# Partial results added by adding transfers instead of on VectorE, and a later start of two lines of dense work, in an FNet and Mish-dense mix

## The chip, the cores and the metric

The kernel runs on one core of a Trainium2 chip. That core has TensorE (PE) for matrix products, VectorE (DVE) for elementwise work, ScalarE (ACT) for copies and activations, GpSimd (POOL) and SyncE (SP), which here only issue transfers between the chip's DRAM and its SBUF, and 16 DMA engines that carry those transfers out. PE writes its sums into PSUM, which has eight banks of 128x512 floats. The metric is the device time of one execution in microseconds (us); less is better.

## The reference

The input is x of 2048 rows (the sequence) by 640 columns. Two branches of it are mixed, row by row, by a gate:

```python
g = _sigmoid((x * gate_w).sum(-1, keepdims=True))
# branch A: real part of a Fourier transform over both axes
a = jnp.einsum("bsd,ed->bse", x, dft_hid_re)
b = jnp.einsum("bsd,ed->bse", x, dft_hid_im)
y = jnp.einsum("ts,bse->bte", dft_seq_re, a) - jnp.einsum("ts,bse->bte", dft_seq_im, b)
# branch B: dense, Mish, dense (640 -> 1728 -> 640)
h = jnp.einsum("bsd,df->bsf", x, w1) + b1
sp = jnp.log1p(jnp.exp(-jnp.abs(h))) + jnp.where(h > 0, h, jnp.zeros_like(h))
act = h * jnp.tanh(sp)
return g * y + (1 - g) * jnp.einsum("bsf,fd->bsd", act, w2)
```

All of it is in float32.

## The kernel before

**Products.** Every matrix product is cut into tiles of 128x128 by 128x512. To keep float32 accuracy each operand is split into a high and a low part: ACT copies the tile into a rounded type (the groups that the profile calls `cut<-flat` on ACT, lines 521 and 529), and DVE subtracts that from the tile to get the rest (`cut<-flat,cut` on DVE, all of whose elementwise work is recorded by line 483). A product is then three matmuls, high by high, high by low and low by high (`mm3`, which calls `mm`; every matmul of the kernel has line 535). Operands that are sums or differences of tiles are built first, on DVE (`flat<-flat`), since the large products are taken in a scheme with fewer products and more additions, of Strassen's kind, at two levels.

**Stages.** The sequence transform is made first, on x itself, as four problems `sq[0]` to `sq[3]`: the even ones (0 and 2) with the real matrix (`in_c_re_dram`) and the odd ones (1 and 3) with the imaginary one (`in_c_im_dram`), and of each pair the first for one half of the result and the second for the other. A problem has a `first`, a `second` and a `third` part. The first parts of all four come ahead. While they run, work of the first dense layer is laid between their steps: two lists of units (`lines`), each unit a few matmuls with `in_w1h_dram` and `in_xt_dram`, an activation and a store. In a loop over the 23 steps of the first parts of problems 2, 3 and 0, the first list gives one piece per step from the first step on, the second from the second step on; what is left of the lists is given behind the loop. Then, for q = 0 to 3, come the second and third part of `sq[q]` and a **second-level unit** (class `Halves`). The units of q = 0 and 1 (`UNITS`) make a sum of their own and hand three tiles of 128x512 on to the problem `sq[q + 2]`, whose own three tiles wait in DRAM (`ps`, its `aside`). The units of q = 2 and 3 (`LOWER`) hand three tiles to `sq[q - 2]`, whose three wait in DRAM too (`pl`, its `lower`). After the four come the gate, the hidden transform (`hd`), the second dense layer (`fin`, `ou`) and the output.

**How a second-level unit adds before the change.** In `Halves.steps`, `self.y(0, t2)` loads a partial tile from DRAM into an SBUF tile (SP issues it), DVE adds the unit's PSUM bank to it (`tt(r21, p4, r21, OP.add)`), the second half of the unit runs, a second PSUM bank is added, and the result is stored by POOL as a tile of `u`, the sequence transform's result in DRAM. Three tiles go this way in each unit (lines 957 to 959 and 992 to 994), so each unit has three loads, three DVE additions that are there for the loaded tile alone, and three stores.

**Adding transfers.** POOL can issue a transfer that adds what it carries to what lies at its destination. The kernel uses it already: `add_in` (line 495) adds a second tile of the Fourier matrix from DRAM to one in SBUF; in the trace these are `flat<-in_c_im_dram` and `flat<-in_c_re_dram` on POOL.

**What sets the order.** Everything is first recorded in a graph and then ordered by a planner (`run`, `order`). PE's order is the order of the code. The orders of DVE, ACT, SP and POOL and the choice of buffers come from the planner, which simulates the engines with its own durations and gives each piece a due time (`want`). Before the change it makes 12 tries from random seeds (`TURNS`), each from the best one so far, and keeps the one in which PE loses least by the plan. Stores and adding transfers all stand in POOL's one queue, and loads in SP's.

```python
def add_in(v, src):
    dma("POOL", lambda: nc.gpsimd.dma_start(v.t, src, accum_op=OP.add), whole(v), whole(v), ADDED * P * N * 4)
```

Of the kernel before, what the change touches and what calls it, by code (L numbers as in the profile page):

```python
# [17 lines left out]
P = 128  # L18
# [25 lines left out]
ADDED = 2.0  # L44
BEHIND = 9
# [29 lines left out]
class Graph:  # L75
# [73 lines left out]
    def run(self, pools):  # L149

        self.wants()
        full = [list(p.free) for p in pools]
        vals = {id(v): v for op in self.ops for v in op.vals}.values()
        left = [v.left for v in vals]
        best = None
        for turn in (None, *TURNS, "last"):
            if best:
                for op, want in zip(self.ops, best[1]):
                    op.want = want
            if best and turn != "last":  # L160
                rng = Random(turn)
                if rng.random() < 0.5:
                    self.adapt(best[2], rng.choice((2.0, 4.0, 8.0)), rng.choice((0.3, 0.6, 1.0)))
                self.hurry(best[2], rng)
            wants = [op.want for op in self.ops]
# [8 lines left out]
            began = self.order(pools, turn == "last")  # L174
            if not began or turn == "last":
                continue
            lost = max(began[op.n] - op.at for op in self.ops if op.engine == "PE")
            if not best or lost < best[0]:
                best = lost, wants, began

    def hurry(self, began, rng):

        def sooner(op, want):
            todo = [(op, want)]
            while todo:
                op, want = todo.pop()
                want = max(want, op.since)
                if op.engine == "PE" or want >= op.want:
                    continue
                op.want = want  # L190
                todo += [(d, want - d.took) for d in op.deps]
        last = None
        for op in self.ops:
            if op.engine != "PE":
                continue
            if last and began[op.n] - began[last.n] > MM + TOLD and rng.random() < 0.7:
# [31 lines left out]
    def order(self, pools, final):  # L228
# [69 lines left out]
        while left:  # L298
            went = False
            for e, line in ready.items():  # L300
# [92 lines left out]
def fnet_mish_gate(ctx: ExitStack, tc: tile.TileContext, xn, xt, c_re, c_im, wd_re, wd_im,  # L393
# [99 lines left out]
    def add_in(v, src):  # L493

        dma("POOL", lambda: nc.gpsimd.dma_start(v.t, src, accum_op=OP.add), whole(v), whole(v), ADDED * P * N * 4)  # L495

# [147 lines left out]
    class Problem:  # L644
# [3 lines left out]
        def __init__(self, st, tp, moving, finish, y=None, q=None, rest=None, aside=None, last=False, apart=None, bare=False, lower=None):  # L648
            self.st, self.moving, self.finish, self.y, self.q = st, moving, finish, y, q
            self.t1, self.t2, self.rest, self.aside, self.last = 2 * tp, 2 * tp + 1, rest, aside, last  # L650
            self.apart, self.bare, self.lower = apart, bare, lower
            self.held, self.kept = {}, [Val(t=dr.tile([P, N], F32, name=f"s2_{next(serial)}")) for k in range(st.kh)]
# [27 lines left out]
        def second(self, low):  # L680
# [10 lines left out]
            for p, k in in_turn(kh, *[("s3", "s2", "s1")] * 2, ends):  # L691
                if ("s3", k) not in own and p == ("s3" if k < kh - 2 else ends[0]):
                    low(k)
                    a22 = self.moving(t2, k + kh)
                    summed = st is seq and k in SUMMED
# [182 lines left out]
    class Halves:  # L878
# [35 lines left out]
        def steps(self):  # L914
# [72 lines left out]
            if not self.into:  # L987
# [4 lines left out]
                f = self.y(4, t2)  # L992
                tt(f, d2, f, OP.add)
# [427 lines left out]
    def put_out(d, t, f, queue=None):  # L1421
# [5 lines left out]
                  lower=aside(f"pl{q}") if q + 2 in LOWER else q in LOWER) for q in range(4)]  # L1427
    hd = [Problem(hid, tp, lambda t, k: load_of(FS, usc[k][t]), put_y, aside=None,
# [33 lines left out]
    for q in range(4):  # L1462
        sq[q].second(seq.low)
        sq[q].third()
        if q in UNITS:
            later = sq[q + 2]
            unit = Halves(seq, 0, 2, lambda t, k: c_tile(q)(t, k + KH), None, sq[q],
                          lambda d, t: load_of(FS, later.aside[min(d, 2)]), later.finish)
# [3 lines left out]
        if q in LOWER:  # L1472
# [3 lines left out]
                          lambda d, t: load_of(FS, there.lower[min(d, 2)]), there.finish, True)  # L1476
# [85 lines left out]
```

## Time and profile before

| | before |
|---|---|
| time, median of 3 runs | 845.81 us (845.71 to 846.83) |
| time of the profiled execution | 847.53 us |
| span of its trace, first to last instruction | 845.8 us |
| granted TensorE clock, mean | 0.999 |

The profiled execution is 1.7 us longer than the median, which is its own variation and what lies around the span; a sum made in its trace is set against 847.53, and its difference carried to 845.81. Engines are named as above; `PEld` is PE's loading of weights, which runs beside its matmuls, `SPq` and `POOLq` are the two queues that issue transfers. A timeline row has the start, the length, the engine, line, operation, output and inputs of a stretch of like instructions, how many (x), and in square brackets how long the engine was idle ahead of it and what ended that. The rows are shown where the prediction uses them.

### The profile page before, as it was taken

To read this page: it belongs to the slowest core of one execution; us is meant where nothing else is said; L and a number is where in the kernel's file an instruction comes from. 1 tells how busy PE (TensorE), PEld (TensorE's weight loads), DVE (VectorE), ACT (ScalarE), POOL (GpSimd) and SP (SyncE) were. 2 spreads that over 40 slices of the span, in tenths; PEclk is the share of its full clock that TensorE was granted. 3 is DMA by queue.
4 is the path that set the end of the run, shared out by engine and by line. 5 is a ranking of instruction groups with operands and counts; after the bars stand their busy time and mean duration, and the time that the engine had idled before them with its cause. 6 is when DMAs were issued, how large, how long until landed. Compare 5 with 4: busy or idle time off the path is not lost.

```text
span 845.8 us, 12270 instructions
## 1 busy us (share of the span) xinstructions
PE 838.9 (99%) x3679; PEld 689.3 (82%) x3679; DVE 759.8 (90%) x1204; ACT 544.3 (64%) x1016; POOL 142.4 (17%) x239
## 2 busy tenths in 40 slices
PE   9999999999999999999999999999999999999998
PEld 6788888878888888888888878888888888888886
DVE  6966989999899999999999999998585899999984
ACT  6966775875475566657658767656576886645442
POOL 0133230112111301220010022012233111011200
PEclk9999999999999999999999999999999999999999
DMA  9979998899789986998667959778799798969963
GB/s 307 354 260 355 324 303 265 273 299 334 231 295 280 349 270 202 301 340 291 181 218 243 328 201 390 228 255 272 251 306 409 268 311 280 341 193 315 301 224 144
DMA packets 120228, 238.77 MB, mean 282 GB/s; under 512 B 15264, under 2 KB 23328, under 8 KB 120160
## 3 DMA queue, kind: packets, MB, share of 16 engines
q1 hardware_dynamic: 98912, 177.80, 62.3%
q0 software_dynamic: 21104, 60.05, 22.9%
q8 instruction: 29, 0.48, 0.2%
q14 instruction: 39, 0.32, 0.1%
q10 hardware_dynamic: 144, 0.13, 0.0%
HBM read 183.64 MB, written 54.28 MB: 281 GB/s over the span
## 4 chain that ended last, share of the span: by engine, by line
PE 71%; DVE 13%; issue 7%; DMA 5%; POOL 2%; SPq 1%; ACT 0%; POOLq 0%; DVEq 0%; ACTq 0%
PE ps L535 71%; DVE cut L483 7%; DVE flat L483 5%; DMA flat<-in_c_re_dram 2%; SPq L456 1%; DMA flat<-in_c_im_dram 1%; DMA flat<-early 1%; POOL act L466 1%; DMA act<-flat 1%; DMA u<-flat 1%; DVE ps L483 1%; DMA flat<-in_xt_dram 1%; POOL flat L495 0%; POOL early L466 0%; POOL t L623 0%
## 5 line engine op out<-in xcount | busy, mean ns | idle before, releaser
L535 PE MATMUL ps<-cut 128*128 128x512 f32 x3671 | 835.4, 389 | 2.0 <-DVE cut L483 0.9
L535 PEld LDWEIGHTS ps<-cut 128*128 128x128 f32 x3671 | 688.3, 188 | 149.5 <-DVE cut L483 2.7
L529 ACT ACTIVATE cut<-flat 128x512 fp32r<-128x512 f32 x499 | 298.8, 627 | 198.1 <-DVE flat L483 122.1
L483 DVE TENSOR_TENSOR cut<-flat,cut 128x512 fp32r<-128x512 f32 (+5 forms) x551 | 400.0, 757 | 28.0 <-ACT cut L529 24.8
L483 DVE TENSOR_TENSOR flat<-flat 128x512 f32<-128x512 f32 (+4 forms) x439 | 281.5, 665 | 9.0 <-DMA flat<-in_c_im_dram 3.4
L509 ACT ACTIVATE flat<-ps 128x512 f32<-128x512 f32 x171 | 99.3, 595 | 49.9 <-PE ps L535 42.4
L483 DVE TENSOR_TENSOR flat<-ps,flat 128x512 f32<-128x512 f32 x123 | 81.3, 685 | 26.6 <-PE ps L535 23.2
L521 ACT ACTIVATE cut<-flat 128x256 fp32r<-128x256 f32 (+4 forms) x190 | 85.0, 478 | 12.8 <-DVE flat L483 8.3
L509 ACT ACTIVATE ps<-flat 128x512 f32<-128x512 f32 x74 | 43.4, 594 | 6.4 <-DVE flat L483 5.1
L466 POOL DMA_DIRECT2D act<-flat x52 | 28.2, 542 | 96.0 <-ACT flat L1018 74.6
L466 POOL DMA_DIRECT2D u<-flat x40 | 22.1, 556 | 108.7 <-ACT flat L509 53.9
L1018 ACT ACTIVATE flat<-flat,b1s 128x512 f32<-128x512 f32 x33 | 23.8, 721 | 12.5 <-DVE flat L483 12.1
L483 DVE TENSOR_TENSOR ps<-ps,flat 128x512 f32<-128x512 f32 x35 | 23.4, 694 | 3.2 <-ACT flat L509 2.1
L495 POOL DMA_DIRECT2D flat<-in_c_im_dram x16 | 14.0, 877 | 68.3 <-DVE cut L483 22.3
L495 POOL DMA_DIRECT2D flat<-in_c_re_dram x16 | 14.4, 922 | 41.7 <-DMA flat<-in_c_re_dram 25.3
L1018 ACT ACTIVATE flat<-ps,b1s 128x512 f32<-128x512 f32 x19 | 13.0, 687 | 8.1 <-PE ps L535 7.0
L471 POOL DMA_DIRECT2D out_dram<-flat x10 | 8.8, 970 | 51.4 <-DMA flat<-act 26.9
L466 POOL DMA_DIRECT2D out_dram<-flat x10 | 5.4, 539 | 51.8 <-DVE flat L483 51.4
L1392 DVE SCALAR_TENSOR_TENSOR flat<-flat 128x640 f32<-128x640 f32 x16 | 13.1, 818 | 0.7 <-DMA flat<-in_xn_dram 0.7
L466 POOL DMA_DIRECT2D s<-flat x12 | 6.5, 546 | 41.4 <-DVE flat L483 21.1
L466 POOL DMA_DIRECT2D y<-flat x10 | 5.4, 540 | 45.4 <-DVE flat L483 44.7
L466 POOL DMA_DIRECT2D early<-flat x12 | 6.7, 562 | 26.0 <-ACT flat L509 11.1
(36 smaller groups left out, 73.3 us busy)
## 6 DMA issues: line engine op xcount, KB each, us to landing
flat<-in_c_im_dram SPq DMA_DIRECT2D x112, 256.0 KB, 5.0
flat<-in_c_re_dram SPq DMA_DIRECT2D x112, 256.0 KB, 4.8
flat<-act SPq DMA_DIRECT2D x88, 256.0 KB, 5.4
flat<-u SPq DMA_DIRECT2D x60, 256.0 KB, 4.9
act<-flat POOLq DMA_DIRECT2D x52, 256.0 KB, 4.7
flat<-in_xt_dram SPq DMA_DIRECT2D x42, 256.0 KB, 4.7
u<-flat POOLq DMA_DIRECT2D x40, 256.0 KB, 5.6
flat<-in_xn_dram SPq DMA_DIRECT2D x24, 320.0 KB, 4.6
```

What stands on the lines that cost most here:

```text
L456: op = dma(queue, lambda: ISSUE[queue].dma_start(v.t[:rows, :cols], src() if callable(src) else src), whole(of) if of else [], whole(v), r ...
L466: dma(queue, lambda: ISSUE[queue].dma_start(d.t, v.t[:rows]), whole(v), whole(d), rows * N * 4)
L471: dma("POOL", lambda: nc.gpsimd.dma_start(o.t, v.t, accum_op=OP.add), whole(v, o), whole(o), 2.8 * P * N * 4)
L483: nc.vector.tensor_tensor(o, a, b, op=alu)
L495: dma("POOL", lambda: nc.gpsimd.dma_start(v.t, src, accum_op=OP.add), whole(v), whole(v), ADDED * P * N * 4)
L509: act(lambda: nc.scalar.activation(o.t, a.t, AF.Copy, scale=scale), whole(a), whole(o))
L521: act(lambda: nc.scalar.activation(w.t[0][:, c], src.t[:, s], AF.Copy), whole(src), hs, n)
L529: act(lambda: nc.scalar.activation(r.t[0][:, :N], src.t[:, :N], AF.Copy), whole(src), [(r, 0)])
L535: G.add("PE", lambda: nc.tensor.matmul(bank.t, w.t[wn][:, k * P:k * P + P], x.t[xn_][:, :N], start, stop, skip_group_check=True), [(w, (k, ...
L1018: act(lambda: nc.scalar.activation(o.t[rows], src.t[rows], AF.Mish, **more), whole(src, table) + whole(b1s) * bias, whole(o), more=0.1)
L1392: dve(lambda k=k, x=x: nc.vector.scalar_tensor_tensor(x.t, x.t, 1.0, wide.t, op0=OP.mult, op1=OP.mult, accum_out=gcol.t[:, k:k + 1]), whol ...
```

## The change

The change has four parts. First, the units of q = 0 and 1 no longer load the partial tile: `self.y` is `None`, ACT copies the PSUM bank to SBUF (`to_sbuf`), and at the end `onto` issues an adding transfer (`add_in` with the DRAM tile as its source) into that SBUF tile, ahead of the store. Second, the unit of q = 2 does not load either: the three tiles of `sq[0]` are stored in their places in `u` from the start, and the unit's results are added to them there by POOL (`add_to_dram`). The unit of q = 3 (`PLAIN`) is as it was. Third, the two lists of first dense units begin at steps 1 and 2 instead of 0 and 1 (`BEGIN`). Fourth, the planner takes the eight new seeds one upon another and uses the last, and counts transfers of the plan's first 60 us as 1.08 times as long (`SLOW`).

```diff
+SLOW = 60.0, 1.08
+BEGIN = 1, 2
-TURNS = (120000, 120002, 120003, 120005, 120008, 120012, 120021, 120029, 120045, 120049, 120056, 120057,)
+TURNS = (700003, 700004, 700006, 700007, 700011, 700013, 700017, 700065)
+PLAIN = (3,)
...
-        for turn in (None, *TURNS, "last"):
...
+        began = again(not TURNS)
+        for turn in TURNS:
+            self.haste(began, turn)
+            began = again(turn == TURNS[-1])
...
-                    dma = max(now + DELAY, dma) + op.moves
+                    dma = max(now + DELAY, dma) + op.moves * (SLOW[1] if now < SLOW[0] else 1)
...
-        o = place(d, t)
+        add_to_dram(place(d, t), v)
+
+    def add_to_dram(o, v):
+
         dma("POOL", lambda: nc.gpsimd.dma_start(o.t, v.t, accum_op=OP.add), whole(v, o), whole(o), 2.8 * P * N * 4)
...
-    def add_in(v, src):
-
-        dma("POOL", lambda: nc.gpsimd.dma_start(v.t, src, accum_op=OP.add), whole(v), whole(v), ADDED * P * N * 4)
+    def add_in(v, src, of=None):
+
+        dma("POOL", lambda: nc.gpsimd.dma_start(v.t, of.t if of else src, accum_op=OP.add),
+            whole(v, of) if of else whole(v), whole(v), ADDED * P * N * 4)
...
-                r21, r22 = self.y(0, t2), self.y(1, t2)
-                tt(r21, p4, r21, OP.add)
-                tt(r22, b, r22, OP.add)
+                if self.y:
+                    r21, r22 = self.y(0, t2), self.y(1, t2)
+                    tt(r21, p4, r21, OP.add)
+                    tt(r22, b, r22, OP.add)
+                else:
+                    r21, r22 = to_sbuf(p4), to_sbuf(b)
...
-                f = self.y(4, t2)
-                tt(f, d2, f, OP.add)
+                if self.y:
+                    f = self.y(4, t2)
+                    tt(f, d2, f, OP.add)
+                else:
+                    f = to_sbuf(d2)
...
-                  lower=aside(f"pl{q}") if q + 2 in LOWER else q in LOWER) for q in range(4)]
+                  lower=(aside(f"pl{q}") if q + 2 in PLAIN else [usc[q % 2 * KD + j][1] for j in (0, 1, 4)]) if q + 2 in LOWER else q in LOWER) for q in range(4)]
...
-        for line in lines if n else lines[:1]:
-            next(line, None)
+        for line, start in zip(lines, BEGIN):
+            if n >= start:
+                next(line, None)
...
-            unit = Halves(seq, 0, 2, lambda t, k: c_tile(q)(t, k + KH), None, sq[q],
-                          lambda d, t: load_of(FS, later.aside[min(d, 2)]), later.finish)
+
+            def onto(d, t, v):
+                add_in(v, None, later.aside[min(d, 2)])
+                later.finish(d, t, v)
+            unit = Halves(seq, 0, 2, lambda t, k: c_tile(q)(t, k + KH), None, sq[q], None, onto)
...
-                          lambda d, t: load_of(FS, there.lower[min(d, 2)]), there.finish, True)
+                          (lambda d, t: load_of(FS, there.lower[min(d, 2)])) if q in PLAIN else None,
+                          there.finish if q in PLAIN else lambda d, t, v: add_to_dram(there.lower[min(d, 2)], v), True)
```

What the planner makes of this is seen in the engines' orders, of which three places follow. Each row is a line of the source, an operation, its output and input, its shape, and how many of it follow one another.

The first place is SP's queue from its 14th transfer (13th after the change) to its 28th, issued before in the first 18 us: loads of Fourier matrix tiles (`in_c_im`, `in_c_re`), of x (`in_xn`) and of the first dense layer's operands (`in_xt`, `in_w1h`). Before:

```order
L456 DMA flat<-in_xn_dram 128x384
L456 DMA flat<-in_xt_dram 128x512 x3
L456 DMA flat<-in_w1h_dram 128x384 x2
L456 DMA flat<-in_c_im_dram 128x512
L456 DMA flat<-in_xt_dram 128x512
L456 DMA flat<-in_w1h_dram 128x384 x2
L456 DMA flat<-in_c_im_dram 128x512
L456 DMA flat<-in_xn_dram 128x384
L456 DMA flat<-in_c_re_dram 128x512 x3
```

And after the change:

```order
L457 DMA flat<-in_c_im_dram 128x512 x2
L457 DMA flat<-in_xt_dram 128x512 x2
L457 DMA flat<-in_w1h_dram 128x384
L457 DMA flat<-in_xt_dram 128x512
L457 DMA flat<-in_xn_dram 128x384
L457 DMA flat<-in_xt_dram 128x512
L457 DMA flat<-in_c_im_dram 128x512
L457 DMA flat<-in_w1h_dram 128x384 x2
L457 DMA flat<-in_xn_dram 128x384
L457 DMA flat<-in_w1h_dram 128x384
L457 DMA flat<-in_c_re_dram 128x512 x3
```

The last `in_c_im` ahead of the three `in_c_re` had four `in_w1h` ahead of it and has one now; the last `in_xn` had four and has three. The `in_xn` before that one, which was the 14th transfer, is the 19th.

The second place is PE at the end of the loop over the first parts, some 100 us into the program, where the rest of the two lists is given out. `ps` and a number is a PSUM bank; a bank's rows are the matmuls that add into it. Before:

```order
L535 MATMUL ps_69<-cut 128x512 x6
L535 MATMUL ps_74<-cut 128x512 x3
L535 MATMUL ps_72<-cut 128x512 x3
L535 MATMUL ps_68<-cut 128x512 x3
L535 MATMUL ps_73<-cut 128x512 x6
L535 MATMUL ps_69<-cut 128x512 x3
L535 MATMUL ps_71<-cut 128x512 x15
```

And after:

```order
L540 MATMUL ps_74<-cut 128x512 x3
L540 MATMUL ps_68<-cut 128x512 x3
L540 MATMUL ps_67<-cut 128x512 x3
L540 MATMUL ps_73<-cut 128x512 x6
L540 MATMUL ps_70<-cut 128x512 x6
L540 MATMUL ps_73<-cut 128x512 x3
L540 MATMUL ps_72<-cut 128x512 x15
```

Before, the bank that six matmuls fill (`ps_69`) is taken up again for three after fifteen others; after the change (`ps_73`) after six others.

The third place is POOL's queue around the end of the unit of q = 0, some 200 us into the program. `u_` and numbers are tiles of the result in DRAM, `ps_` and a number partial tiles in DRAM. Before:

```order
L495 DMA flat<-in_c_im_dram 128x512 x4
L466 DMA u_0_78<-flat 128x512
L466 DMA u_0_94<-flat 128x512
L466 DMA u_2_80<-flat 128x512
L466 DMA u_2_84<-flat 128x512
L466 DMA u_2_96<-flat 128x512
L466 DMA u_0_82<-flat 128x512
L495 DMA flat<-in_c_im_dram 128x512 x4
```

And after:

```order
L499 DMA flat<-in_c_im_dram 128x512 x4
L467 DMA u_0_78<-flat 128x512
L467 DMA u_0_94<-flat 128x512
L499 DMA flat<-in_c_im_dram 128x512
L499 DMA flat<-ps_251 128x512
L499 DMA flat<-ps_252 128x512
L499 DMA flat<-ps_253 128x512
L467 DMA u_0_82<-flat 128x512
L499 DMA flat<-in_c_im_dram 128x512
L467 DMA u_2_80<-flat 128x512
L467 DMA u_2_84<-flat 128x512
L499 DMA flat<-in_c_im_dram 128x512
```

The second group of four additions to the Fourier tiles is taken apart: its first two have changed places, and the one that PE needs first, the first of the four before, now stands behind one other such addition, the three new adding transfers and one store, with the three stores that they feed behind it.

More of the change, by code (lines that the diff above doesn't have):

```diff
@@ L44 @@
 ADDED = 2.0
+SUMMED_HID = 0
+PLAIN = (3,)
 BEHIND = 9
@@ L154, in run, with again @@
         left = [v.left for v in vals]
-        best = None
-        for turn in (None, *TURNS, "last"):
[L157 to L165, printed above, removed]
+        def again(final):
             for p, free in zip(pools, full):
@@ L173, in run, with haste, hurry @@
                 op.mate = None
[L174 to L181, printed above, removed]
+            return self.order(pools, final)
+        began = again(not TURNS)
+        for turn in TURNS:
+            self.haste(began, turn)
+            began = again(turn == TURNS[-1])
+    def haste(self, began, turn):
+        rng = Random(turn)
+        if rng.random() < 0.5:
+            self.adapt(began, rng.choice((2.0, 4.0, 8.0)), rng.choice((0.3, 0.6, 1.0)))
+        self.hurry(began, rng, 0.7)
+    def hurry(self, began, rng, share):
         def sooner(op, want):
@@ L195, in hurry @@
                 continue
-            if last and began[op.n] - began[last.n] > MM + TOLD and rng.random() < 0.7:
+            if last and began[op.n] - began[last.n] > MM + TOLD and rng.random() < share:
                 o, by = op, rng.choice((0.5, 1.0, 2.0, 4.0, 8.0))
@@ L651, in __init__ @@
             self.apart, self.bare, self.lower = apart, bare, lower
+            self.summed = SUMMED if st is seq else range(SUMMED_HID) if st is hid and not tp else ()
             self.held, self.kept = {}, [Val(t=dr.tile([P, N], F32, name=f"s2_{next(serial)}")) for k in range(st.kh)]
@@ L694, in second @@
                     a22 = self.moving(t2, k + kh)
-                    summed = st is seq and k in SUMMED
+                    summed = k in self.summed
                     if summed:
@@ L1426, in fnet_mish_gate @@
                   apart=UNITS and q % 2 in UNITS, bare=q - 2 in UNITS,
[L1427 to L1428 removed]
+                  lower=(aside(f"pl{q}") if q + 2 in PLAIN else [usc[q % 2 * KD + j][1] for j in (0, 1, 4)]) if q + 2 in LOWER else q in LOWER) for q in range(4)]
+    hd = [Problem(hid, tp, lambda t, k, v=None: add_in(v, None, usc[k][t]) if v else load_of(FS, usc[k][t]), put_y, aside=None,
                   q=lambda t: keep(("g", t), lambda: broadcast(grow, t))) for tp in range(2)]
```

## The prediction

> **What bounds the kernel now.** I begin with the page's first lines, for the share of each engine.
>
> ```profile
> span 845.8 us, 12270 instructions
> PE 838.9 (99%) x3679; PEld 689.3 (82%) x3679; DVE 759.8 (90%) x1204; ACT 544.3 (64%) x1016; POOL 142.4 (17%) x239
> ```
>
> PE is busy 99% of the span, so the question is how much PE loses and where. The timeline of PE lists its unbroken stretches; a stretch of the chain of waits from 275 us on gives its pace when nothing is late.
>
> ```profile
> 0.78 3.57 PE L1370 MATMUL ps<-const-bfloat16-1.0 128*128 128x512 bf16 x8 [0.78 <-PEq L1550]
> 4.39 6.76 PE L535 MATMUL ps<-cut 128*128 128x512 f32 x28
> 11.38 10.27 PE L535 MATMUL ps<-cut 128*128 128x512 f32 x44 [0.23 <-DVE cut L483]
> 21.98 1.12 PE L535 MATMUL ps<-cut 128*128 128x512 f32 x2 [0.33 <-ACT cut L521]
> 23.82 151.93 PE L535 MATMUL ps<-cut 128*128 128x512 f32 x669 [0.71 <-DVE cut L483]
> 176.03 323.80 PE L535 MATMUL ps<-cut 128*128 128x512 f32 x1425 [0.28 <-ACT flat L509]
> 500.08 341.61 PE L535 MATMUL ps<-cut 128*128 128x512 f32 x1503 [0.26 <-ACT flat L509]
> 274.98 25.16 PE ps L535 x111
> ```
>
> 111 matmuls in 25.16 us is 0.2267 us each. The stretches hold 3671 matmuls, 832.2 us at that pace; begun at 4.39 they would end at about 836.8 (the last one's own pipeline adds 0.16), and they end at 500.08 + 341.61 = 841.69. So PE loses **4.9 us in all**, 0.58% of the time: no change that leaves PE its matmuls can win more, and this one leaves all 3671. From start to start the loss is, stretch by stretch: 0.64 up to 11.38 (6.99 us for 28); 0.63 up to 21.98 (10.60 for 44) and 1.39 up to 23.82 (1.84 for 2), together 2.02 at **the start**; 0.55 up to 176.03; 1.00 up to 500.08; 0.72 from there on. Shorter waits within the long stretches show in the loading of weights, which stands idle far beyond its usual gap:
>
> ```profile
> 183.65 1.47 PEld L535 LDWEIGHTS ps<-cut 128*128 128x128 f32 x7 [0.44 <-DVE cut L483]
> 193.08 0.99 PEld L535 LDWEIGHTS ps<-cut 128*128 128x128 f32 x5 [0.24 <-DVE cut L483]
> 501.74 1.23 PEld L535 LDWEIGHTS ps<-cut 128*128 128x128 f32 x6 [0.43 <-ACT flat L509]
> 621.27 0.76 PEld L535 LDWEIGHTS ps<-cut 128*128 128x128 f32 x4 [0.41 <-DVE flat L483]
> ```
>
> Thus of the 1.00 up to 500.08 some 0.45 lies at 183.65 and 193.08 and 0.55 at 500.08 itself; the 0.72 lies at 501.74 and 621.27. DVE, busy 90%, is what ends most of these waits, but they are short: it is a second bound, not the first.
>
> **The change, part by part.**
>
> *The nine additions.* The groups by line give the prices:
>
> ```profile
> L535 PE MATMUL ps<-cut 128*128 128x512 f32 x3671 | 835.4, 389 | 2.0 <-DVE cut L483 0.9
> ...
> L529 ACT ACTIVATE cut<-flat 128x512 fp32r<-128x512 f32 x499 | 298.8, 627 | 198.1 <-DVE flat L483 122.1
> ...
> L483 DVE TENSOR_TENSOR flat<-ps,flat 128x512 f32<-128x512 f32 x123 | 81.3, 685 | 26.6 <-PE ps L535 23.2
> ...
> L509 ACT ACTIVATE flat<-ps 128x512 f32<-128x512 f32 x171 | 99.3, 595 | 49.9 <-PE ps L535 42.4
> ...
> L509 ACT ACTIVATE ps<-flat 128x512 f32<-128x512 f32 x74 | 43.4, 594 | 6.4 <-DVE flat L483 5.1
> ```
>
> Three units lose three DVE additions each, 9 x 0.685 = 6.2 us of DVE, and ACT gains nine copies, 9 x 0.595 = 5.4 us at 64% load. Nothing of this lies on PE's path by itself, since PE is unbroken beside nearly all of it. It is worth something only at waits on DVE that come later: 0.72 at 501.74 and 621.27 (the first names ACT, whose copies there wait in turn on DVE's sums; I count it in). The waits at 176.03, 183.65 and 193.08 (0.55 + 0.45) lie ahead of the first removed addition and can only move by the new plan. The 0.55 at 500.08 is a copy from a bank that PE has just filled, in code that the change leaves: it stays. I take 0.7 for the later waits, half of the 1.0 for the earlier, and give back 0.2 for waits that a new plan makes elsewhere: **-1.0**, between -1.7 (all gone) and +0.3 (none gone, some new).
>
> *The start.* The loss of 2.02 is the last pair of a Fourier tile and an x tile of the first part, which come late:
>
> ```profile
> 11.69 0.97 SPq L456 DMA_DIRECT2D flat<-in_w1h_dram  x2
> ...
> 13.92 0.97 SPq L456 DMA_DIRECT2D flat<-in_w1h_dram  x2
> 15.26 0.33 SPq L456 DMA_DIRECT2D flat<-in_c_im_dram  x1
> 15.90 0.33 SPq L456 DMA_DIRECT2D flat<-in_xn_dram  x1
> ...
> DMA packets 2684, 4.21 MB, mean 351 GB/s; under 512 B 422, under 2 KB 1267, under 8 KB 2684
> ...
> flat<-in_c_im_dram SPq DMA_DIRECT2D x3, 256.0 KB, 4.7
> ...
> 21.87 1.89 DVE L483 TENSOR_TENSOR cut<-flat,cut 128x512 fp32r<-128x512 f32 x5
> ```
>
> The tile issued at 15.26 lands 4.7 us later, at about 20.0, the x tile at about 20.5; ACT's cuts follow, and DVE's for the x tile is the last of the five in the row at 21.87, done at 23.76, when PE goes on. In the new order the Fourier tile has one `in_w1h` load ahead of it instead of four, the x tile three instead of four. At 351 GB/s, 192 KB take 0.56 us, so the first comes 1.7 us sooner, the second 0.56; fewer small dense cuts stand ahead of the x tile's on DVE, since dense work begins a step later. The x tile still lands at about 19.9, and its ACT cut, DVE cut and what stands between reach PE about 1.0 us sooner than now: I take **-1.0**, between -0.4 (only the sooner x tile) and -2.0 (all of it). Against it stands the x tile of the step before, now the 19th load: the load in that place is the second in the row at 11.69, issued by 12.7 and landed near 17, while PE is held up only by the last pair, at 21.3, so I cost it at nothing; if that cover is gone, the gain at the start shrinks with it. The 0.64 at 11.38 stays, since the first twelve loads are the same.
>
> *The later start of the two lists* leaves more for the end of the loop, near 106 us. There a bank is summed on DVE, set again by ACT and filled on by PE. The chain is a matmul from issue to end, 0.389 by its group, the DVE sum, 0.685, and the ACT copy, 0.594: 1.67 us. PE had fifteen other matmuls meanwhile, 3.4 us; it has six, 1.36, and with the last one's own slot 1.59. Bare, that is 0.1 short; with three hand-overs I take **+0.35**, from +0.1 to +0.9 if DVE has just begun another 0.685 us instruction.
>
> *The adding transfers.* The first row below is the share of the DMA engines in use, in tenths, from 198 to 222 us; then come the two queues in 212.6 to 223.2, where just three adding transfers ran beside loads, the time from issue to landing of such transfers from 180 to 230, and rows of POOL and DVE.
>
> ```profile
> DMA  9999999999999999999899999999999999999999
> ...
> q1 hardware_dynamic: 1348, 2.45, 63.7%
> q0 software_dynamic: 432, 0.79, 40.3%
> ...
> DMA to landing us min/median/max: 5.5/6.9/7.5
> ...
> 205.68 0.91 POOL L495 DMA_DIRECT2D flat<-in_c_im_dram  x1 [1.56 <-DMA flat<-in_c_im_dram]
> ...
> 204.84 0.81 DVE L1392 SCALAR_TENSOR_TENSOR flat<-flat 128x640 f32<-128x640 f32 x1
> ...
> 215.61 1.89 DVE L483 TENSOR_TENSOR cut<-flat,cut 128x512 fp32r<-128x512 f32 x3
> ```
>
> An adding transfer takes 40.3% of 10.6 us by three, 1.42 us of all 16 DMA engines; a load (2.45 MB is 9.35 tiles) 0.72. In each of units 0 and 1 three loads (-2.2) give way to three adds (+4.3); in unit 2 three loads and three stores give way to three adds, which is nothing. So the chip's DMA has 4.2 us more to do, most of it where it is already full, around 200 to 220. The place that counts is the Fourier addition issued at 205.68, landed by the median at 212.6. It now stands behind four adds that stood behind it or were not there (+5.7) and ahead of three stores (-2.2); the three loads are gone (-2.2); and POOL may reach it up to 1.7 sooner. That puts it at 212.2 to 213.9, and I take 213.2. Behind it come ACT's cut, 0.63, and in DVE's queue some six instructions that follow each other at 0.60 (the row at 215.61) and two of the gate at 0.74: 5.7 us, so PE's matmul can go at 218.9. It is the 190th behind the one at 176.03 and due at 219.5 (190 x 0.2267 and 0.4 for the waits at 183.65 and 193.08), or some 0.6 sooner after the gains ahead: 218.9. It is a tie, and I take **+0.5** from 0 to +2.3, and **+0.1** for units 1 and 2, where PE ran unbroken beside the additions (the row at 274.98), with up to +0.5.
>
> The Trainium skill, "DMA: Bandwidth & Descriptors", section "Issuing engines are not separate DMA queues", speaks against this part: transfers started by any engine run on the same 16 DMA engines and interleave, so a second queue saves only the time of issuing. The trace agrees: 63.7% and 40.3% share one whole. By that page the adds could only delay the loads, which would be the slower rival below.
>
> **The sum** is -1.0 - 1.0 + 0.35 + 0.5 + 0.1 = -1.05 us. Made in the profiled execution, 847.53 with a span of 845.8, it would give 846.5; the median of the runs shown is 1.7 lower, which I take as that execution's own variation around the same steps. Carried to the median, 845.81 - 1.05 is **844.8**.
>
> **The rivals.**
>
> *Covers hold and the gaps close.* The start gains 1.7, the drain costs 0.2, the adds nothing, the other waits give 1.4: -2.9, **842.9**. For it: DVE has 6.2 us less to do from 200 us on and fewer dense cuts at the start; PE waits on DVE in five of the nine waits shown. Against it: the x tile comes only 0.56 sooner.
>
> *It does not matter.* PE is at 99% and the removed work lay beside it; the plan trades one small wait for another. Start -0.5, drain +0.4, adds +0.3, rest -0.2: **845.8**. For it speaks that each of the losses is below 2.1 us and of its own cause.
>
> *Slower: the Fourier addition behind the adds.* If it lands past 213.2 on POOL's queue, each further us is PE's. With no earlier issue and half the relief from the three loads it lands at 215.0 (212.6 + 5.7 - 2.2 - 1.1), so +1.8; the same arrangement in unit 1, where PE had more lead, adds 0.7; the drain at 0.9 and a start that gains 0.9 cancel, and the rest gives nothing: +2.5, **848.3**. Against it: three of the loads that crowd this place are gone.
>
> **How the numbers follow.** I give the forecast 0.38 (844.0 to 845.7), the closed gaps 0.30, no matter 0.20, the late addition 0.12. A measurement of this kernel can tell about 0.2%, 1.69 us: below 844.12 is faster, above 847.50 slower. The closed gaps lie below the first bound and a sliver of the forecast's (0.04) does: **faster 0.34**; the rest of it and the third case: **same 0.54**; **slower 0.12**. The ends of all terms add up to -3.6 and +3.6; with about a tenth left out on each side the range is **842.8 to 847.3**.
>
> **What would show it.** PE's timeline of the changed kernel should have one loss near 22 us, of about 1 us instead of 2.02, a small new one near 105 us with ACT's copy to a bank as its end, no waits near 621, and the one near 500 as before. Near 219 it has a wait of 0 to 1 us that DVE's cut ends; 2 us there is the slower rival. The DVE group `flat<-ps,flat` should count nine fewer and ACT's `flat<-ps` nine more. I am wrong if a loss of over 1 us stands at a place not named here, or if the last x tile of the start comes no sooner.

## The result and the profile after

The changed kernel takes **854.06 us** (median of 4 runs, 853.03 to 855.58) against 846.32 for the kernel before in the same session (845.71 to 847.52): a ratio of 1.0091 with a 95% interval of 1.0068 to 1.0114. The forecast was 844.8, in a range that ended at 847.3. The sign was wrong, and the time lies outside the range.

The profiled execution took 855.58, with a span of 853.8; it is the slowest of the four. First the timeline of PE of the changed kernel, with the columns of the one shown of before:

```profile
4.52 17.20 PE L540 MATMUL ps<-cut 128*128 128x512 f32 x74 [0.17 <-DVE cut L532]
22.08 135.71 PE L540 MATMUL ps<-cut 128*128 128x512 f32 x594 [0.36 <-DVE cut L487]
158.00 0.96 PE L540 MATMUL ps<-cut 128*128 128x512 f32 x3 [0.22 <-ACT flat L514]
159.12 16.61 PE L540 MATMUL ps<-cut 128*128 128x512 f32 x72
177.60 45.00 PE L540 MATMUL ps<-cut 128*128 128x512 f32 x190 [1.87 <-ACT flat L514]
225.28 169.47 PE L540 MATMUL ps<-cut 128*128 128x512 f32 x738 [2.68 <-DVE cut L487]
395.18 454.51 PE L540 MATMUL ps<-cut 128*128 128x512 f32 x2000 [0.43 <-DVE cut L487]
```

At 0.2267 us a matmul the stretches can be read as before. Start to start, PE loses 0.78 in the first stretch (17.56 us for 74), 1.26 up to 158.00, 0.44 up to 159.12, **2.16** up to 177.60, **4.61** up to 225.28, **2.60** up to 395.18 and 0.95 to the end, and it begins 0.13 later: 12.9 us where the kernel before lost 4.9. The difference is the 8.0 us by which the span grew. The waits at 177.6 and 225.3 are 2.0 and 2.85 us from matmul to matmul, but the stretches that follow them lose too. The windows view, with PE's busy time, its matmuls in brackets and its granted clock in the column after POOL's, shows how:

```profile
177.60:178.80 1.20, 1.20 (x5) 1.03 (x6) 1.20 (x4) 0.46 (x2) 0.00 (x0) 1.00 1.06 348
178.80:182.20 3.40, 3.40 (x10) 2.47 (x10) 3.40 (x6) 3.35 (x7) 0.60 (x1) 0.52 1.05 360
225.20:226.80 1.60, 1.52 (x6) 1.24 (x7) 1.60 (x4) 0.26 (x1) 0.00 (x0) 0.98 1.08 384
226.80:230.20 3.40, 3.40 (x10) 2.65 (x9) 3.20 (x7) 2.07 (x4) 0.00 (x0) 0.51 0.97 300
```

After each of the two waits PE works for 1.2 to 1.5 us at full clock and then for 3.4 us at half: 8 matmuls at 0.427 us, some 1.6 us lost. So the wait at 177.6 costs 3.8 us in all and the one at 225.3 costs 4.5, together 8.3; new small waits near 158 (0.9) and 395 (1.0) make it 10.2, and 2.2 are gained elsewhere. These are PE's losses by place, and not what mending one place alone would bring: PE that comes sooner to the second place can wait longer there (keep_warm, below).

What ended the wait at 225.3 stands in the chain of waits of the changed kernel (start, length, what):

```profile
211.57 12.20 DMA flat<-in_xn_dram
223.76 0.02 issue
223.78 0.83 DVE flat L1404 x2
224.62 0.62 DVE cut L487
225.23 0.04 issue
225.28 9.85 PE ps L540 x35
```

A load of x for the gate, issued at 211.57, took 12.2 us to land; DVE's gate instruction waits for it and the cut that PE needs stands behind. DVE's timeline shows that this was the last of several hold-ups in its queue:

```profile
218.91 0.69 DVE L487 TENSOR_TENSOR cut<-flat,cut 128x512 fp32r<-128x512 f32 x1 [2.74 <-ACT cut L534]
219.52 0.82 DVE L1404 SCALAR_TENSOR_TENSOR flat<-flat 128x640 f32<-128x640 f32 x1
...
220.49 1.42 DVE L487 TENSOR_TENSOR flat<-flat 128x512 f32<-128x512 f32 x2
...
223.78 0.83 DVE L1404 SCALAR_TENSOR_TENSOR flat<-flat 128x640 f32<-128x640 f32 x1 [1.27 <-DMA flat<-in_xn_dram]
```

The 2.74 us ahead of 218.91 are the wait for the Fourier addition of k = 4. The row at 220.49 begins 0.02 us after the landing of a plain load of a Fourier tile, which SP issued at 209.31 and which took 11.2 us. So with these two loads landing when they did, DVE would have come to the cut no sooner had the addition been on time. POOL's timeline says why the addition was late:

```profile
204.13 3.00 POOL L499 DMA_DIRECT2D flat<-ps  x3
205.80 1.90 POOL L467 DMA_DIRECT2D u<-flat  x1
206.36 2.25 POOL L499 DMA_DIRECT2D flat<-in_c_im_dram  x1
```

The view of its source line from 206.3 to 207 has the time from issue to landing, of it (the longest) and of the last of the three:

```profile
DMA to landing us min/median/max: 9.8/10.8/11.8
```

Issued at 206.36, behind the three adding transfers of the unit, it needed 11.8 us and landed at 218.2. The prediction had it at 213.2. The loads of SP's queue that were issued behind the adding transfers were late with it.

### The profile page after: what moved, and what is told of

Same layout as the page of the kernel before. It is cut to its first block, busy times and chain, and to the rows that moved or that the text cites. A ratio compares the mean times of both kernels' runs of the same rounds, so it can differ in the third digit from the quotient of the medians.

```text
span 853.8 us, 12295 instructions
## 1 busy us (share of the span) xinstructions
PE 842.8 (99%) x3679; PEld 691.4 (81%) x3679; DVE 755.9 (89%) x1192; ACT 551.9 (65%) x1025; POOL 149.4 (17%) x245
## 4 chain that ended last, share of the span: by engine, by line
PE 78%; DVE 10%; DMA 6%; issue 3%; ACT 2%; SPq 1%; DVEq 0%; ACTq 0%; POOLq 0%
PE ps L540 78%; DVE cut L487 5%; DVE flat L487 4%; DMA flat<-in_xn_dram 3%; DMA flat<-in_c_re_dram 2%; DMA flat<-in_c_im_dram 1%; ACT cut L534 1%; SPq L457 1%; ACT flat L514 1%; DMA flat<-in_xt_dram 1%; ACT flat L1030 0%; DVE flat L1404 0%; DVE ps L487 0%; ACT ps L514 0%; ACT cut L526 0%
## 5 line engine op out<-in xcount | busy, mean ns | idle before, releaser
L487 DVE TENSOR_TENSOR cut<-flat,cut 128x512 fp32r<-128x512 f32 (+6 forms) x566 | 403.4, 743 | 33.1 <-ACT cut L534 29.1
L514 ACT ACTIVATE flat<-ps 128x512 f32<-128x512 f32 x180 | 104.4, 595 | 46.1 <-PE ps L540 39.8
L526 ACT ACTIVATE cut<-flat 128x128 fp32r<-128x128 f32 (+4 forms) x190 | 84.4, 479 | 25.9 <-DVE flat L487 20.6
L487 DVE TENSOR_TENSOR flat<-ps,flat 128x512 f32<-128x512 f32 x114 | 75.3, 686 | 24.2 <-PE ps L540 17.7
L467 POOL DMA_DIRECT2D u<-flat x40 | 25.2, 632 | 163.7 <-ACT flat L514 78.1
L499 POOL DMA_DIRECT2D flat<-in_c_im_dram x16 | 15.8, 986 | 52.4 <-DMA flat<-in_c_im_dram 31.3
```

The source lines that it names most:

```text
L467: dma(queue, lambda: ISSUE[queue].dma_start(d.t, v.t[:rows]), whole(v), whole(d), rows * N * 4)
L487: nc.vector.tensor_tensor(o, a, b, op=alu)
L499: dma("POOL", lambda: nc.gpsimd.dma_start(v.t, of.t if of else src, accum_op=OP.add), whole(v, of) if of else whole(v), whole(v), ADDED * ...
L514: act(lambda: nc.scalar.activation(o.t, a.t, AF.Copy, scale=scale), whole(a), whole(o))
L526: act(lambda: nc.scalar.activation(w.t[0][:, c], src.t[:, s], AF.Copy), whole(src), hs, n)
```

## The experiments

Two of them (thin_adds, keep_warm) keep the changed kernel's order on every engine, row by row in their traces. The three that begin with `hold` move a few transfers, and the planner's last pass then also lays the work behind them otherwise. The other three let the planner draw the whole order anew. Times are medians; the ratio is to the kernel before on the same chip, whose median was 846.43 in the first four and 846.8 in the others.

**thin_adds**: each of the six adding transfers of units 0 and 1 carries 128 of its 512 columns.

```diff
-        dma("POOL", lambda: nc.gpsimd.dma_start(v.t, of.t if of else src, accum_op=OP.add),
+        dma("POOL", lambda: nc.gpsimd.dma_start(v.t[:, :P] if of else v.t, of.t[:, :P] if of else src, accum_op=OP.add),
```

> The changed kernel with the same order on every engine, but each of the six adding transfers of units 0 and 1 carries 128 of its 512 columns (three quarters of the partial tiles are not added, so the output differs). Theory A, the price of the adding transfers: their 1.42 us each of the DMA engines, at 204 to 215 us where these are full, makes the loads and the Fourier addition behind them late, and that is PE's wait of 2.85 us at 222.2 with the half-speed matmuls after it (1.6). With a third of the price the wait falls below 0.5 us, the half-speed matmuls go with it, and the time is about 4.3 us below the changed kernel's 854.1, near 849.7. Theory C, the new plan alone: the wait at 222 stays within 0.5 us, near 853.5. Both leave the wait at 175.3 as it is (2.0).

848.25 us (10 runs), ratio 1.0021 (1.0011 to 1.0032). PE's timeline has at this place

```profile
175.09 2.33 PE L540 MATMUL ps<-cut 128*128 128x512 f32 x9 [0.79 <-ACT flat L514]
...
219.35 167.75 PE L540 MATMUL ps<-cut 128*128 128x512 f32 x738 [0.23 <-DVE cut L487]
```

The wait of 2.85 us is 0.4 (218.72 to 219.35 from matmul to matmul), and no half-clock matmuls follow. The same chain ends it: the gate's load of x, issued at 208.67, took 9.2 us here instead of 12.2. With every order untouched, the size of the adding transfers makes the wait: theory A holds, and the plan alone does not make it. The wait at 175 was 0.95 here, below its 2.0 and without half-clock matmuls behind it, with the same order ahead of it; it differs from run to run. The time fell by 5.8 us, more than the 4.3 expected, and this first wait lies ahead of all that the edit shrinks.

**hold_adds4**: the same adding transfers at full size, but in POOL's queue behind the Fourier additions of k = 4 to 7. The planner's last pass holds three transfers back. Its orders are the changed kernel's up to that place. Behind it they are not, other than the text below expects: by the traces, SP's differs from the transfer that the changed kernel issues at 211.57 on, DVE's from its row at 215.48, ACT's from 244.74.

```diff
+                        if final and o.behind and not set(o.behind) <= began.keys():
+                            continue
...
+    for o in brought[:3]:
+        o.behind = [fourier[i].n for i in range(12, 16)]
```

> The changed kernel with one difference in POOL's queue alone: the three adding transfers of unit 0 are issued behind the Fourier additions of k = 4 to 7 instead of ahead of three of them. Theory B, the order in the queue: the Fourier addition of k = 4 lands near 211 instead of 218.2, the gate's loads come sooner too, the wait at 222.2 falls from 2.85 to under 0.5 us, time near 849.7. Theory A alone (it is the sum of DMA work at this place, whatever its order): at least 1.5 us of the wait stays there or comes within the next 15 us, time 852 or more. The wait at 175.3 stays.

847.34 us (10 runs), ratio 1.001 (1.000 to 1.002), 6.7 us below the changed kernel. PE's timeline, and POOL's where the wait had been:

```profile
177.28 2.33 PE L546 MATMUL ps<-cut 128*128 128x512 f32 x9 [1.19 <-ACT flat L520]
179.98 327.40 PE L546 MATMUL ps<-cut 128*128 128x512 f32 x1438 [0.37 <-ACT ps L520]
```

```profile
204.74 0.87 POOL L502 DMA_DIRECT2D flat<-in_c_im_dram  x1
...
215.44 3.01 POOL L502 DMA_DIRECT2D flat<-ps  x3
```

PE is unbroken from 180 to 507. The Fourier addition of k = 4 is issued 1.6 us earlier and lands within 6.1 us, at 210.8; the three adding transfers follow at 215.4. The loads of x for the gate come sooner too; in the DMA view of 198 to 224 us they show first for the changed kernel, then for this one, with their number, size and median time to landing:

```profile
flat<-in_xn_dram SPq DMA_DIRECT2D x3, 320.0 KB, 10.0
```

```profile
flat<-in_xn_dram SPq DMA_DIRECT2D x3, 320.0 KB, 4.8
```

All the DMA work is still done, so its amount alone does not make the wait; **its order** does: theory B. How much of this is the place of the three transfers in POOL's queue, and how much the other order of SP and DVE behind them, this run does not separate. The kernel is level with the one before. More than the 4.4 us of the expectation went: the wait at 177.3 is 1.35 us here, not 2.0, and no half-clock matmuls follow it; it lies ahead of all that the edit moves, and is not its doing.

**hold_adds1**: the three behind the Fourier addition of k = 4 alone (`range(12, 13)` in the diff above).

> As hold_adds4, but the three adding transfers of unit 0 go behind the Fourier addition of k = 4 alone, so those of k = 6 and 7, and the gate's two loads that SP issues at 208.7 and 211.6 us, stay behind them. If the Fourier addition of k = 4 alone is what PE waits for at 222.2, the wait goes as with hold_adds4 (time 847 to 848). If the gate's loads, which DVE's queue has ahead of the cuts that PE needs, make the larger part, a wait of 1 to 2.5 us stays within 5 us of that place, with DVE idle for a load of x ahead of the gate's instruction (time 849 to 852).

851.23 us (4 runs), ratio 1.0062 (1.0039 to 1.0085). PE's timeline:

```profile
176.20 45.15 PE L546 MATMUL ps<-cut 128*128 128x512 f32 x190 [1.97 <-ACT flat L520]
222.03 270.12 PE L546 MATMUL ps<-cut 128*128 128x512 f32 x1190 [0.68 <-DVE cut L490]
```

The wait at 222 falls from 2.85 to 0.96 and does not go: between the two expectations. DVE's timeline shows that the fall is not the Fourier addition's alone:

```profile
219.35 1.42 DVE L490 TENSOR_TENSOR flat<-flat 128x512 f32<-128x512 f32 x2 [1.15 <-DMA flat<-in_c_im_dram]
220.69 1.28 DVE L490 TENSOR_TENSOR cut<-flat,cut 128x512 fp32r<-128x512 f32 x2
222.52 0.83 DVE L1410 SCALAR_TENSOR_TENSOR flat<-flat 128x640 f32<-128x640 f32 x1 [0.55 <-DMA flat<-in_xn_dram]
```

In the new plan the gate instruction stands behind the cuts that PE needs, where it stood ahead of the last of them. Its load of x, which SP now issues one Fourier load later, landed only at 222.5; that Fourier load landed at 221.25. With the gate instruction ahead again, and the 1.5 us that lay there between its start and PE's (223.78 to 225.28), PE would have waited some 1.7 us with the load of x at 221.25 and 2.9 with it at 222.5; this is an estimate. What is left of the wait ends with a plain load of a Fourier tile, issued at 207.89, that took 11.4 us. So the late loads of SP's queue hold PE too, and not the Fourier addition alone. The rest of the 851.23 is the wait at 176.2, 2.1 us in this run, with half-clock matmuls, and new waits near 493, 1.4 us.

**keep_warm**: twelve matmuls with zero weights, which add nothing, in PE's idle time ahead of the two waits (4 and 8).

```diff
+            emit()
+            for _ in range(n):
+                nc.tensor.matmul(v.t, zeros, ones, False, False, skip_group_check=True)
...
+    fill(pe[742], 4)
+    fill(pe[932], 8)
```

> The changed kernel with the same order on every engine, but twelve more matmuls on PE, of zero weights, which add nothing: four behind the last matmul ahead of the wait at 175.3 us and eight behind the last ahead of the wait at 222.2. They stand in time that PE spends waiting, so the waits still end when they did, but PE is idle for about 1.1 us in each instead of 2.0 and 2.85. Theory D, the clock: it is idling of some 2 us that halves TensorE's pace for the next 3.4 us (seven to eight matmuls at 0.427); then no matmul behind the two waits takes 0.427, and the time is 1.6 to 3.1 us below the changed kernel's, 851 to 852.5. If the half pace has another cause (late weights or operands), the slow matmuls stay and the time is that of the changed kernel, 853 to 855.

851.67 us (4 runs), ratio 1.0063 (1.0045 to 1.0081), 2.4 us below the changed kernel. The windows behind the two waits:

```profile
178.80:182.20 3.40, 3.02 (x13) 2.15 (x13) 3.40 (x5) 2.88 (x6) 0.90 (x1) 1.00 0.96 338
227.00:230.20 3.20, 3.20 (x16) 2.63 (x15) 3.00 (x7) 2.15 (x4) 0.00 (x0) 1.00 0.94 294
```

The clock stays at 1.00, with 13 and 16 matmuls where there were 10. Theory D holds: idling itself brings the half clock. The gain in time is that of the median: in the profiled execution, the slowest of the four with 854.81, PE came sooner to the second place and waited 1.43 and 3.11 us there instead of 2.85. The Trainium skill, "TensorE: Matmul & The Clock Gate", section "Part 1: The HAM clock gate", describes this gate: half rate after an idle window of about 3.4 us, full rate after as long a busy one. The 3.4 us at half clock behind the changed kernel's two waits agree with the page; that idling of 2.0 us was enough here does not fit its 3.4, and the measurement decides.

**no_adds** and **adds_only** split the change in two: the new planner and the later start with the old loads and DVE additions, and the adding transfers with the old planner, seeds and start.

```diff
-PLAIN = (3,)
+PLAIN = (2, 3)
...
+                          lambda d, t: load_of(FS, later.aside[min(d, 2)]), later.finish)
```

> The changed kernel without its adding transfers: units 0 to 2 load their partial tiles and add them on DVE as before; the new planner, the new seeds and the later start of the dense lists stay. Theory C (the new plan makes the wait at 175.3): a wait of 1 to 2.5 us stays between 155 and 180, the one at 222 is gone, time 848 to 851. If the adding transfers make both waits, it is at 844.5 to 846.5. Every order is planned anew, so a wait may also move.

> The kernel before with the adding transfers of units 0 to 2 alone: its planner, its seeds and the start of its dense lists are those of before. Theory A: a wait of over 1.5 us near 220, no long wait near 175, time 848 to 851. Theory C: no wait of over 1 us anywhere behind 30 us, time 845 to 847. Every order is planned anew.

Both missed. no_adds takes 855.31 us, ratio 1.0102 (1.0087 to 1.0118), adds_only 854.02, ratio 1.0083 (1.0066 to 1.01), and neither has its long waits where a theory put them. PE's timeline of no_adds, then of adds_only:

```profile
94.45 18.45 PE L540 MATMUL ps<-cut 128*128 128x512 f32 x69 [3.61 <-ACT flat L514]
...
509.20 3.72 PE L540 MATMUL ps<-cut 128*128 128x512 f32 x15 [1.30 <-ACT ps L514]
```

```profile
96.93 405.62 PE L543 MATMUL ps<-cut 128*128 128x512 f32 x1781 [2.17 <-DVE flat L490]
504.40 0.50 PE L543 MATMUL ps<-cut 128*128 128x512 f32 x1 [1.85 <-ACT cut L537]
506.47 342.55 PE L543 MATMUL ps<-cut 128*128 128x512 f32 x1502 [1.57 <-DVE cut L490]
```

In adds_only the adding transfers also stand ahead of the Fourier addition of k = 4, and PE does not wait there, though it comes to that place at 222.2 us as in the changed kernel. The addition lands at 216.9 there, 1.3 us sooner, and DVE has no gate instruction between that landing and PE's matmul. So the place in POOL's queue does not make the wait by itself: what DVE's order has behind it decides too. The two halves do not price the parts of the change: every graph is planned anew, and a plan brings its own waits of 2 to 4 us.

**before_seeds** tests that: the kernel before with the changed kernel's eight seeds, and nothing else.

```diff
-TURNS = (120000, 120002, 120003, 120005, 120008, 120012, 120021, 120029, 120045, 120049, 120056, 120057,)
+TURNS = (700003, 700004, 700006, 700007, 700011, 700013, 700017, 700065)
```

> The kernel before with nothing changed but the planner's seeds, for which the eight of the changed kernel stand: what is computed, the transfers and the additions are those of before, only the orders differ. If a plan of the same graph is worth under 1 us either way, the time is 845 to 847. If the plan by itself moves the time as no_adds and adds_only suggest (waits of 2 to 4 us at places that the plan does not see), it is 848 to 856.

854.1 us (4 runs), ratio 1.0084 (1.0062 to 1.0107): as slow as the change, with the same work as before in another order. PE's timeline has, among others,

```profile
15.87 0.50 PE L535 MATMUL ps<-cut 128*128 128x512 f32 x1 [0.90 <-ACT cut L529]
17.13 159.97 PE L535 MATMUL ps<-cut 128*128 128x512 f32 x697 [0.76 <-DVE cut L483]
...
506.29 341.81 PE L535 MATMUL ps<-cut 128*128 128x512 f32 x1500 [1.67 <-ACT cut L521]
```

and half-clock matmuls follow 17.13 and 506.29. The order is worth as much as all that was changed.

**hold_swap**: hold_adds4 and, for the wait at 175 to 178, one exchange in SP's queue. That wait lies 26 us ahead of the first adding transfer, so these cannot make it. ACT's timeline of the changed kernel has

```profile
170.27 1.15 ACT L534 ACTIVATE cut<-flat 128x512 fp32r<-128x512 f32 x2 [2.01 <-DMA flat<-in_c_re_dram]
```

ACT waits 2.0 us for a tile of the real Fourier matrix, issued at 164.14 behind a load of x whose buffer came free late, and DVE, SP and PE wait in turn. Against hold_adds4 the orders of all engines but SP stay the same, and in SP's this one load moves.

```diff
+    G.ops[1467].behind = [1535]
```

> hold_adds4, and in SP's queue one load of the real Fourier matrix, issued at 164.1 us, goes ahead of the load of x before it, whose buffer comes free 3 to 4 us later. Theory E, the order in SP's queue: ACT and DVE waited for that Fourier tile (landed at 170.2), and PE's wait at 175.3 is what came of it; the tile lands 3 to 5 us sooner, the wait (1.35 in hold_adds4) falls below 0.4, time about 1.2 us below hold_adds4, 845.5 to 846.5, at or a little below the kernel before. Rival: the place is short of SBUF buffers whatever the order; the wait stays over 0.8 or moves within 20 us, time as hold_adds4, 847.3.

846.70 us (11 runs), ratio 1.000 (0.9991 to 1.0009). The exchanged load goes out at 161.6, ACT's cut of it starts at 166.07 instead of 170.27, and PE's timeline becomes

```profile
106.93 69.77 PE L546 MATMUL ps<-cut 128*128 128x512 f32 x305 [0.19 <-ACT ps L520]
177.07 327.35 PE L546 MATMUL ps<-cut 128*128 128x512 f32 x1438 [0.37 <-ACT ps L520]
504.64 336.46 PE L546 MATMUL ps<-cut 128*128 128x512 f32 x1481 [0.22 <-DVE cut L490]
```

The wait there is 0.2 us (173.93 to 174.37); theory E holds for the wait, which is 0.95 to 2.1 us in the five profiles with the old order at this place (after the change, thin_adds, keep_warm, hold_adds4, hold_adds1). The time is 0.2 us above the expected range, and the 0.6 us that separate it from hold_adds4 are not clear of the noise. By moving four transfers in two queues, and with what the planner then lays otherwise, the changed kernel is brought back to the time of the kernel before, 7 us down, and no further: its nine removed DVE additions and its better start are paid for by the small waits at 106.9, 177.1 and 504.6. None of the kernels measured beats the one before.

## Why the prediction was wrong

*The bound* was read rightly: PE has 3671 matmuls at 0.2267, and all that a change can do shows as losses between them. The same view accounts for the 8 us after. What was drawn from it was lopsided: 4.9 us bounds what can be won, and nothing bounds what can be lost, so a range of -3.0 to +1.5 us around 845.8 was too narrow on the far side.

*The nine additions* count as said. The groups by line of the changed kernel:

```profile
L514 ACT ACTIVATE flat<-ps 128x512 f32<-128x512 f32 x180 | 104.4, 595 | 46.1 <-PE ps L540 39.8
...
L487 DVE TENSOR_TENSOR flat<-ps,flat 128x512 f32<-128x512 f32 x114 | 75.3, 686 | 24.2 <-PE ps L540 17.7
```

Nine copies more and nine sums less, at the same 0.595 and 0.685 us each. Of the 0.7 us that this was to bring at the waits behind 500, about 0.3 came (0.95 us lost from 395 on, against 0.55 + 0.72 from 500 on).

*The start* came as forecast: two waits, 0.63 us ending at 22.08 and 0.37 at 24.3, where 2.02 had been lost, -1.0. The last Fourier tile went out at 12.96 instead of 15.26 and the last x tile at 14.98 instead of 15.90, so the reason was right too. The 0.64 at 11.38, which was to stay, went as well, for 0.4 at the first matmul (0.13 by which it begins later, 0.24 behind it).

*The later start of the lists* cost what was forecast, +0.35: in the changed kernel PE waits for ACT's copy at 107.39, 0.22 and 0.11 in the slot after; hold_swap's row at 106.93 shows the same wait.

*The adding transfers* are where the forecast failed, at the step "the three loads are gone (-2.2)". SP's timeline of the kernel before shows when those three loads were issued:

```profile
175.02 0.48 SPq L456 DMA_DIRECT2D flat<-ps  x1
...
176.07 0.38 SPq L456 DMA_DIRECT2D flat<-ps  x1
...
184.66 2.25 SPq L456 DMA_DIRECT2D flat<-ps  x2
```

The three are the rows at 175.02 and 176.07 and the first of the two at 184.66; the changed kernel still issues three other loads of `ps` at 185 to 190. They had gone out 20 to 30 us ahead of the crowded stretch, so their going relieved nothing there, while an adding transfer can only be issued when the unit's result is ready, at 204, in the midst of it. Without that relief the working gives 212.6 + 5.7 - 2.2 = 216.1, and measured was 218.2: the addition was issued at 206.36, 0.7 later than before and not up to 1.7 sooner, and the three adding transfers and those behind them landed 1.1 to 2.1 us apart, where 1.42 had been counted for an addition and 0.72 for a store. The second omission is that only the Fourier addition was followed. All the loads behind the adding transfers were late: a plain Fourier load landed at 220.5 and the gate's x at 223.8, and DVE has both ahead of the cut that PE needs. The last of them ended the wait, and not the addition. The third is the clock: the wait was priced at its own length, and at 2.85 us it cost 1.6 more. In place of +0.5 the place cost 4.5. The nearest rival, the Fourier addition behind the adds, had the right place and 12% of the chance; it too followed the addition alone, and its +1.8 was too small for the same reasons.

The rule of the Trainium skill that was weighed ("DMA: Bandwidth & Descriptors", section "Issuing engines are not separate DMA queues"), that transfers of all issuing engines run on the same 16 DMA engines, was borne out, and it deserved more than a sentence beside the sum: with the adding transfers at a quarter of their size and every order the same, the gate's load of x, which stands in another engine's queue, took 9.2 us instead of 12.2.

*The earlier waits* were to lose half of 1.0 us by the new plan. Instead they became 3.8 at 177.6 and 0.9 near 158. That was the other failed step: "half of the 1.0 for the earlier", a guess that a new plan is as likely to be better. before_seeds shows the sort of draw it was: the order of the kernel before is a good one, and another for the same work costs 7 us.

## What to carry to other kernels

A load that is replaced by an adding transfer is not the same transfer made cheaper or dearer: the load can be made long ahead, the adding transfer only when its other addend is ready, so price it at the time when it must run, and ask which transfers will queue behind it. When a change makes a planner draw a new order for a kernel that is bound at 99%, the order is part of the change and can cost more than the edit; separate the two by keeping the order and moving a few instructions, and compare the orders of all engines in the traces, since holding back three transfers moved others here. And a wait of PE of 1.9 us or more cost more than its length in these runs.

## What the runs showed of the hardware

By the idle time in brackets, waits of PE of 1.87 us and more were followed by half clock wherever they stood alone (1.87 and 2.68 in the changed kernel, 1.97 in hold_adds1, 2.17 in adds_only, 3.61 in no_adds), waits of 1.19 and 1.30 us were not (hold_adds4, no_adds); and two waits of 0.90 and 0.76 us with a single matmul between them were (before_seeds, at 17.13). So the idle share over a few us seems to count, and in these profiles the change for a single wait lies between 1.3 and 1.9 us. The half clock sets in up to 1.5 us after work has begun again. Behind the two waits of the changed kernel it lasts 3.4 us, 1.6 us lost each time; behind the 3.61 of no_adds it lasts 5.3 us, 2.6 us lost.

The start can show the same pace, and it is not in the granted clock: in the profile of hold_adds4 the first Fourier tile landed at 4.36 instead of 3.79 in the kernel before, the first matmul comes at 4.96 instead of 4.39, nine matmuls then stand 0.427 us apart, and the windows view shows 10 matmuls in 4.4 us where the kernel before has 23 in 5.0, both at a clock of 1.00:

```profile
4.90:9.30 4.40, 4.34 (x10) 3.46 (x11) 4.18 (x8) 3.70 (x7) 0.00 (x0) 1.00 1.03 380
```

```profile
4.30:9.30 5.00, 4.96 (x23) 4.07 (x23) 3.39 (x6) 2.21 (x4) 0.00 (x0) 1.00 1.00 340
```

The profile of adds_only has the same, with its first matmul at 4.93; the other profiles, where it comes at 4.39 to 4.56, do not. So half a microsecond by which this load lands later goes with a loss of over 2 us, and may be why ten runs of hold_adds4 spread from 846.35 to 849.9; neither the cause of the half pace nor that of the spread was tested.
